# Second feed-forward: h blocks of two chunks by seven products in place of eight

## The chip, the core and the metric

The kernel runs on one core of a Trainium2 chip. The metric is the time of one execution on the device in microseconds (us). Engines: TensorE (PE, with its weight loads as PEld), VectorE (DVE), ScalarE (ACT), GpSimd (POOL) and SyncE (SP), which here issues nearly all DMAs, on one queue.

## The reference, cut to what matters

```python
attn_out = _attn_ref(q, k, v, i_gate, f_gate, o_gate)     # 4 batches, 8 heads, 768 steps, 40 wide
x = attn_out.transpose(0, 2, 1, 3).reshape(3072, 320)
x = (sigmoid(x @ w_gate) * (x @ w_val)) @ w_out           # first feed-forward, 1536 wide
h = x @ w_in                                              # second feed-forward, 2048 wide
g = h * clip(h + 3, 0, 6) / 6
return g @ w_out2                                         # all in float32
```

The change touches `h = x @ w_in` alone, and what has to be at hand for it.

## The kernel before, in words

The 768 steps are cut into 6 chunks of 128; one chunk holds the 512 tokens of four batches. The matmuls take float32 in a form (fp32r) that keeps part of the bits, so each operand is split into a high part (a ScalarE cast) and a low part (a VectorE subtraction), and a product is made of high x high, high x low and low x high.

The first part of the program runs 82 steps, chunk by chunk. Each step computes an h block of the first feed-forward (`m1_h`, 512 columns, L553 to L560), then the output product of the step before (`outputs_but`, `m1_out`), and one piece of the attention of the next chunk (`att0`, `att1`, `att2`). The first two chunks are cut into half blocks; chunks 3 to 6 have 12 steps each, and the sixth has no attention beside it. What VectorE does in a step: the product of gate and value (L580), the low split (L567), and of the attention the decay scans (L387), the weighing (L402) and the outputs' scaling. `work` adds jobs to the steps: it fetches weights as 64-bit words, turns them into float32 (`to_f32`: ScalarE, then VectorE L117 and L120) and, for the second feed-forward, stores them in DRAM (`store_w2`, w2_dram). In the sixth chunk and the first part of the second feed-forward `work` loads them again and splits them into SBUF slots: `split_in` for the h product, `split_out2` for the output product.

The second feed-forward (L844 to L858) runs over 6 chunks and, in each, 8 blocks of two times 128 features. `m2_h(c, n)` makes 2 x 8 matmuls of 512 columns (two blocks of 128 rows with three terms each, the tail of 64 rows in two matmuls) into two PSUM banks of the pool mm_ps; the gate is a ScalarE Relu (L806) and a VectorE product with h (L807), then comes the split (L566, L567). `m2_out(c, n - 1)` follows: 24 matmuls of 320 columns into four banks that sum over all features. `x_split(c + 1)` loads the next chunk's x from x2_dram and splits it.

The eight PSUM banks are three of mm_ps, three of acc_ps and two of att_ps. A planner in the framework orders each engine's instructions when the program is built: by the order in which they are written, and by when their inputs and buffers come free by its own estimates. At run time each engine takes its instructions in that fixed order; so does the DMA queue of SP, where a store that waits for its data holds up the loads behind it. `issue_after(gate)` keeps what is written in it behind that step's gate on the gate's engine.

## Time and profile before

| | |
|---|---|
| runs | 868.65, 869.58 and 872.16 us, median 869.58 |
| profiled execution, first to last instruction | 867.3 us (its span; 2.3 us less than the median) |
| TensorE busy | 842.9 us, 97% |
| VectorE busy | 497.8 us, 57% |
| ScalarE busy | 353.3 us, 41% |
| moved by DMA | 83.4 MB |

The page gives busy shares in 40 slices of the span (about 21.7 us each), the chain of work that ended last, and groups of instructions with their mean duration. Durations of matmuls overlap: the next starts before the last has ended. The windows give each engine's busy time in a stretch; time in which two instructions of one engine overlap counts once there.

### The profile page before, as it was taken

To read this page: it belongs to the slowest core of one execution; us is meant where nothing else is said; L and a number is where in the kernel's file an instruction comes from. 1 tells how busy PE (TensorE), PEld (TensorE's weight loads), DVE (VectorE), ACT (ScalarE), POOL (GpSimd) and SP (SyncE) were. 2 spreads that over 40 slices of the span, in tenths; PEclk is the share of its full clock that TensorE was granted. 3 is DMA by queue.
4 is the path that set the end of the run, shared out by engine and by line. 5 is a ranking of instruction groups with operands and counts; after the bars stand their busy time and mean duration, and the time that the engine had idled before them with its cause. 6 is when DMAs were issued, how large, how long until landed. Compare 5 with 4: busy or idle time off the path is not lost.

```text
span 867.3 us, 16991 instructions
## 1 busy us (share of the span) xinstructions
PE 842.9 (97%) x7205; PEld 727.1 (84%) x7205; DVE 497.8 (57%) x898; ACT 353.3 (41%) x721; POOL 2.5 (0%) x8
## 2 busy tenths in 40 slices
PE   6599899999999999999999999999999999999998
PEld 6488689888878887878888888999999999999997
DVE  8899975765666666667535544344343343443432
ACT  3687743232333343342225445343343343433332
POOL 1000000000000000000000000000000000000000
PEclk9599999999999999999999999999999999999999
DMA  9636723422544555344104221001020020000000
GB/s 350 236 123 212 255 73 109 145 73 73 199 133 157 170 184 186 122 163 169 32 1 149 90 68 73 1 31 37 1 68 1 1 67 1 31 1 1 31 1 30
DMA packets 24923, 83.43 MB, mean 96 GB/s; under 512 B 2576, under 2 KB 5840, under 8 KB 24848
## 3 DMA queue, kind: packets, MB, share of 16 engines
q1 hardware_dynamic: 24800, 82.26, 27.7%
q8 instruction: 56, 0.92, 0.4%
q14 instruction: 19, 0.16, 0.0%
q10 hardware_dynamic: 48, 0.10, 0.0%
HBM read 68.35 MB, written 13.99 MB: 95 GB/s over the span
## 4 chain that ended last, share of the span: by engine, by line
PE 92%; DVE 5%; DMA 1%; issue 1%; ACT 0%; DVEq 0%
PE mm L557 12%; PE mm L559 12%; PE mm L558 12%; PE acc L595 11%; PE mm L553 7%; PE mm L560 6%; PE acc L827 5%; PE acc L826 5%; PE acc L825 5%; PE acc L605 4%; PE att L361 3%; PE att L454 2%; PE att L443 2%; PE att L827 2%; PE att L825 2%; PE att L826 2%
## 5 line engine op out<-in xcount | busy, mean ns | idle before, releaser
L557 PE MATMUL mm<-xh,w 128*128 128x512 f32 (+1 forms) x520 | 195.5, 376 | 0.0
L559 PE MATMUL mm<-xh,w 128*128 128x512 f32 (+1 forms) x520 | 194.8, 375 | 0.0
L558 PE MATMUL mm<-xl,w 128*128 128x512 f32 (+1 forms) x520 | 194.7, 374 | 0.0
L566 ACT CAST gh<-g 128x512 fp32r<-128x512 f32 (+1 forms) x178 | 106.0, 596 | 193.5 <-DVE g L580 98.5
L567 DVE TENSOR_TENSOR gl<-g,gh 128x512 fp32r<-128x512 f32 (+1 forms) x178 | 117.5, 660 | 94.5 <-ACT gh L566 93.5
L807 DVE SCALAR_TENSOR_TENSOR g<-g,mm 128x512 f32<-128x512 f32 x96 | 65.8, 685 | 133.8 <-ACT g L806 133.8
L806 ACT ACTIVATE g<-mm,half 128x512 f32<-128x512 f32 x96 | 65.8, 685 | 133.0 <-PE mm L560 132.9
L559 PEld LDWEIGHTS mm<-xh,w 128*128 128x128 f32 x520 | 98.1, 189 | 18.7
L558 PEld LDWEIGHTS mm<-xl,w 128*128 128x128 f32 x520 | 98.1, 189 | 18.5
L557 PEld LDWEIGHTS mm<-xh,w 128*128 128x128 f32 x520 | 98.3, 189 | 14.2
L553 PE MATMUL mm<-xl,w 128*128 128x512 f32 (+1 forms) x260 | 104.0, 400 | 2.5 <-DVE cst L524 1.6
L595 PE MATMUL acc<-gh,w 128*128 128x512 f32 (+1 forms) x328 | 104.0, 363 | 0.0
L560 PE MATMUL mm<-xh,w 128*128 128x512 f32 (+1 forms) x260 | 97.2, 374 | 0.0
L827 PE MATMUL acc<-w,gl 128*128 128x320 f32 x288 | 89.0, 309 | 0.0
L826 PE MATMUL acc<-w,gh 128*128 128x320 f32 x288 | 88.9, 309 | 0.0
L825 PE MATMUL acc<-w,gh 128*128 128x320 f32 x288 | 88.8, 308 | 0.0
L580 DVE TENSOR_TENSOR g<-g,mm 128x512 f32<-128x512 f32 (+1 forms) x82 | 50.5, 616 | 61.9 <-PE mm L560 61.9
L579 ACT ACTIVATE g<-mm 128x512 f32<-128x512 f32 (+1 forms) x82 | 44.6, 544 | 69.1 <-PE mm L560 67.6
L595 PEld LDWEIGHTS acc<-gh,w 128*128 128x128 f32 x328 | 60.4, 189 | 9.9
L387 DVE TENSOR_TENSOR_SCAN dec<-dec,ident 128x512 f32<-128x512 f32 x40 | 48.2, 1217 | 26.7 <-DMA dec<-fz_dram 26.7
L595 PE MATMUL acc<-gl,w 128*128 128x512 f32 (+1 forms) x164 | 59.7, 364 | 0.0
L553 PEld LDWEIGHTS mm<-xl,w 128*128 128x128 f32 x260 | 49.1, 189 | 12.2 <-DVE cst L524 2.0
(155 smaller groups left out, 1077.8 us busy)
## 6 DMA issues: line engine op xcount, KB each, us to landing
raw<-in_w SPq DMA_DIRECT2D x20, 640.0 KB, 4.1
qk<-in_qkT SPq DMA_DIRECT2D x22, 512.0 KB, 4.4
vko<-in_vko SPq DMA_DIRECT2D x22, 480.0 KB, 4.6
dec<-fz_dram SPq DMA_DIRECT2D x20, 512.0 KB, 5.8
raw<-in_wo SPq DMA_DIRECT2D x14, 640.0 KB, 4.0
w_dram<-bits SPq DMA_DIRECT2D x16, 320.0 KB, 2.4
raw<-w_dram SPq DMA_DIRECT2D x16, 320.0 KB, 2.9
x_dram<-x SPq DMA_DIRECT2D x6, 768.0 KB, 3.2
```

Source lines behind the costliest of these rows:

```text
L553: nc.tensor.matmul(out=banks[j], lhsT=tail, rhs=xl[:, 2, :], start=True, stop=False)
L557: nc.tensor.matmul(out=banks[j], lhsT=hi, rhs=xh[:, k, :], start=False, stop=False)
L558: nc.tensor.matmul(out=banks[j], lhsT=hi, rhs=xl[:, k, :], start=False, stop=False)
L559: nc.tensor.matmul(out=banks[j], lhsT=lo, rhs=xh[:, k, :], start=False, stop=False)
L560: nc.tensor.matmul(out=banks[j], lhsT=tail, rhs=xh[:, 2, :], start=False, stop=True)
L566: nc.scalar.copy(out=gh, in_=g)
L567: nc.vector.tensor_tensor(out=gl, in0=g, in1=gh.bitcast(F32), op=ALU.subtract)
L595: nc.tensor.matmul(out=a[m], lhsT=lhsT, rhs=rhs, start=st and lhsT is hi and rhs is gh, stop=en and lhsT is lo, skip_group_check=True,)
L806: nc.scalar.activation(out=g[j], in_=banks[j], func=AF.Relu, scale=1.0 / 6.0, bias=half)
L825: nc.tensor.matmul(out=a, lhsT=gh[:, ts], rhs=hi, start=st, stop=False)
L826: nc.tensor.matmul(out=a, lhsT=gh[:, ts], rhs=lo, start=False, stop=False)
L827: nc.tensor.matmul(out=a, lhsT=gl[:, ts], rhs=hi, start=False, stop=en)
```

## The change

For a pair of chunks and two feature blocks, h is a 2 x 2 matrix of blocks: feature block by chunk. The 320 rows of the contraction are cut into two halves of 160 (128 and a tail of 32). Strassen's scheme, in Winograd's form, makes the four blocks from 7 products of sums of blocks in place of 8 products of blocks. A product is 4 matmuls: three for the 128 rows, and one for the tail, whose four terms stand on four groups of 32 rows.

- `combine_w2` makes the sums of the weights and their splits on VectorE and ScalarE, once for each of the 8 blocks, at odd steps of the fourth and fifth chunk, and stores them (1.38 MB a block) in ws_dram. `load_group` loads them for each pair of chunks again: 24 loads.
- `x_load` and `x_combine` load the x of two chunks and make its sums and splits, in a main and a tail part: for the first pair in the sixth chunk of the first feed-forward, for the others in the second half of the pair before. `x_split` is gone, and the splits of w_in (`split_in`) with it.
- The order of the second feed-forward becomes: for each of 3 pairs, 8 blocks with 7 products each and the output product of the pair's first chunk between them; then the second chunk's 16 output blocks, whose gated values have been kept in the slots that w_in held.
- The first and the third product are copied from PSUM by ScalarE, and further products are added to them there by the matmuls (bank px or pw, accumulating) and by VectorE (`add_to`). The banks come from `four`: three of a pool and one of att_ps in turn.
- Pools of the first part are closed before the sixth chunk, and a pool `late` takes their room.

```diff
...
+    ws_dram = dram.tile([F2 // 2, P, 7, 3 * P], F32, name="ws_dram")
...
-    def x_split(c):
-        x2 = xpool.tile([P, 3, T], F32, tag="x2", name="x2")
-        nc.sync.dma_start(out=x2, in_=x2_dram[c])
-        x_tiles((2, c))
-        nc.scalar.copy(out=XH[2, c], in_=x2)
-        nc.vector.tensor_tensor(
-            out=XL[2, c], in0=x2, in1=XH[2, c].bitcast(F32), op=ALU.subtract
-        )
...
-    for n in range(F2):
+    for n in [*range(0, F2, 2), *range(1, F2, 2)]:
         jobs.append(((wo2 if n % 2 else w2)[n // 2], store_w2, n))
-    n_conv = len(jobs)
-    for n in range(F2):
-        key = ("out2" if n % 2 else "in2", n // 2)
-        jobs.append((w2_dram[n], split_out2 if n % 2 else split_in, key))
     jobs.reverse()
     def work(count, limit):
...
+    def load_out2(n):
+        x = xpool.tile([P, 640], F32, tag="x2", name="w2f")
+        nc.sync.dma_start(out=x, in_=w2_dram[2 * n + 1])
+        split_out2(("out2", n), x)
+    A11, A12, A21, A22, S1, S2, S4 = range(7)
+    S3 = A21
+    def combine_w2(n):
+        src = w2_dram[2 * n]
+        a = cpool.tile([P, 7, 2, P], F32, tag="wa", name="wa", bufs=1)
+        nc.sync.dma_start(
+            out=a[:, 0:4, 0, :], in_=src[:, 0:512].rearrange("p (ik c) -> p ik c", c=P)
+        )
+        tail = src[:, 512:640].rearrange("(ik r) c -> r ik c", r=32)
+        for r in range(0, P, 32):
+            nc.sync.dma_start(out=a[r : r + 32, 0:4, 1, :], in_=tail)
+        for to, x, y, op in (
+            (S1, A21, A22, ALU.add),
+            (S2, S1, A11, ALU.subtract),
+            (S3, A11, A21, ALU.subtract),
+            (S4, A12, S2, ALU.subtract),
+        ):
+            nc.vector.tensor_tensor(out=a[:, to], in0=a[:, x], in1=a[:, y], op=op)
+        for k, m in ((0, 4), (4, 3)):
+            st = xpool.tile([P, 4, 3, P], F32R, tag="x2", name="ws")
+            sf = st.bitcast(F32)
+            nc.scalar.copy(out=st[:, :m, 0:3:2, :], in_=a[:, k : k + m])
+            nc.vector.tensor_tensor(
+                out=st[:, :m, 1, :], in0=a[:, k : k + m, 0, :], in1=sf[:, :m, 0, :], op=ALU.subtract
+            )
+            for r in (32, 96):
+                q = slice(r, r + 32)
+                nc.vector.tensor_tensor(
+                    out=st[q, :m, 2, :], in0=a[q, k : k + m, 1, :], in1=sf[q, :m, 2, :],
+                    op=ALU.subtract,
+                )
+            nc.sync.dma_start(
+                out=ws_dram[n, :, k : k + m, :],
+                in_=sf[:, :m].rearrange("p s t c -> p s (t c)"),
+            )
+    w_groups = []
+    def load_group(n):
+        t = xpool.tile([P, 7, 3, P], F32R, tag="x", name="wg")
+        nc.sync.dma_start(
+            out=t.bitcast(F32).rearrange("p s t c -> p s (t c)"), in_=ws_dram[n]
+        )
+        w_groups.append(t)
...
+    xsets = []
+    combined = 0
+    def x_load(pair):
+        def rows():
+            return late.tile([P, T], F32, tag="c", name="xr", bufs=11)
+        main, tail = {}, {}
+        for k in range(2):
+            for j in range(2):
+                src = x2_dram[2 * pair + j]
+                main[k, j], tail[k, j] = rows(), None
+                nc.sync.dma_start(out=main[k, j], in_=src[:, k, :])
+        return pair, main
+    def x_combine(loads, tail):
+        pair, b = loads
+        if tail:
+            b = {}
+            for k in range(2):
+                for j in range(2):
+                    b[k, j] = late.tile([P, T], F32, tag="c", name="xr", bufs=11)
+                    for r in range(0, P, 32):
+                        nc.sync.dma_start(
+                            out=b[k, j][r : r + 32],
+                            in_=x2_dram[2 * pair + j, 32 * k : 32 * k + 32, 2, :],
+                        )
+        else:
+            xsets.append(
+                {
+                    key: late.tile([P, 3, T], F32R, tag="X", name="X", bufs=7)
+                    for key in ("B11", "B21", "T1", "T2", "B22", "T3", "T4")
+                }
+            )
+        xs = xsets[-1]
+        b11, b12, b21, b22 = b[0, 0], b[0, 1], b[1, 0], b[1, 1]
+        def put(key, v):
+            x = xs[key]
+            xf = x.bitcast(F32)
+            if tail:
+                nc.scalar.copy(out=x[:, 2, :], in_=v)
+                nc.vector.tensor_tensor(
+                    out=x[64:, 2, :], in0=v[64:], in1=xf[64:, 2, :], op=ALU.subtract
+                )
+            else:
+                nc.scalar.copy(out=x[:, 0, :], in_=v)
+                nc.vector.tensor_tensor(out=x[:, 1, :], in0=v, in1=xf[:, 0, :], op=ALU.subtract)
+        def minus(x, y, out=None):
+            out = late.tile([P, T], F32, tag="c", name="xr", bufs=11) if out is None else out
+            nc.vector.tensor_tensor(out=out, in0=x, in1=y, op=ALU.subtract)
+            return out
+        put("B11", b11)
+        put("B21", b21)
+        t1 = minus(b12, b11)
+        put("T1", t1)
+        t2 = minus(b22, t1)
+        put("T2", t2)
+        put("B22", b22)
+        put("T3", minus(b22, b12, b12))
+        put("T4", minus(b21, t2))
...
             with tc.issue_after(gate):
-                work(c > 1 and f % 2 == 0, n_conv)
+                work(c > 1 and f % 2 == 0, n_jobs)
+                if c > 2 and f % 2 and combined < F2 // 2:
+                    combine_w2(combined)
+                    combined += 1
         elif f == 0:
-            work(F2, n_conv)
+            assert not jobs and not pieces and combined == F2 // 2
+            early_sb.close()
+            late = ctx.enter_context(tc.tile_pool(name="late", bufs=1, reuse_waits="tile"))
+            x_loads = x_load(0)
+            load_group(0)
         else:
-            work(f > 1, n_jobs)
-        if c == NC - 1 and f == 6:
-            x_split(0)
+            if f > 1 and f - 2 < F2 // 2:
+                load_out2(f - 2)
+            if f in (2, 5):
+                x_combine(x_loads, f > 2)
+    taken = [0]
+    def four(odd):
+        taken[0] += 1
+        return ps_att() if taken[0] % 4 == 0 else (ps_acc if odd else ps_mm)()
+    def product(ps, w, s, x, first):
+        for i, (a, b) in enumerate(((2, 2), (0, 1), (1, 0), (0, 0))):
+            nc.tensor.matmul(
+                out=ps, lhsT=w[:, s, a, :], rhs=x[:, b, :], start=first and i == 0, stop=i == 3,
+                skip_group_check=True,
+            )
+    def sbuf_copy(ps):
+        t = late.tile([P, T], F32, tag="c", name="c", bufs=11)
+        nc.scalar.copy(out=t, in_=ps)
+        return t
+    def add_to(t, ps):
+        nc.vector.tensor_tensor(out=t, in0=ps, in1=t, op=ALU.add)
+        return t
+    def gate2(g, h):
+        nc.scalar.activation(out=g, in_=h, func=AF.Relu, scale=1.0 / 6.0, bias=half)
+        nc.vector.scalar_tensor_tensor(
+            out=g, in0=g, scalar=1.0, in1=h, op0=ALU.min, op1=ALU.mult
+        )
+    def gated_split(h):
+        g = gpool.tile([P, T], F32, tag="g", name="g")
+        gate2(g, h)
+        return split_g(g)
     acc2 = {}
-    def m2_h(c, n):
-        banks = [ps_mm(), ps_mm()]
-        h_pair(slots["in2", n], (2, c), banks)
-        gs[c, n] = []
-        g = [gpool.tile([P, T], F32, tag="g", name="g") for _ in range(2)]
-        for j in range(2):
-            nc.scalar.activation(out=g[j], in_=banks[j], func=AF.Relu, scale=1.0 / 6.0, bias=half)
-            nc.vector.scalar_tensor_tensor(
-                out=g[j], in0=g[j], scalar=1.0, in1=banks[j], op0=ALU.min, op1=ALU.mult
-            )
-        for j in range(2):
-            gs[c, n].append(split_g(g[j]))
-    def m2_out(c, n):
-        if n == 0:
-            acc2[c] = [ps_acc(), ps_acc(), ps_acc(), ps_att()]
+    def m2_out(c, n, j, gg):
+        if n == 0 and j == 0:
+            acc2[c] = [(ps_mm, ps_acc)[(c // 2 + c) % 2 ^ 1]() for _ in range(3)] + [ps_att()]
         w = slots["out2", n]
-        gg = gs.pop((c, n))
-        for j in range(2):
-            gh, gl = gg[j]
-            hi, lo = w[:, j, 0:320], w[:, j, 320:640]
-            st, en = n == 0 and j == 0, n == F2 // 2 - 1 and j == 1
-            for t in range(B):
-                ts = slice(t * L, (t + 1) * L)
-                a = acc2[c][t][:, :DM]
-                nc.tensor.matmul(out=a, lhsT=gh[:, ts], rhs=hi, start=st, stop=False)
-                nc.tensor.matmul(out=a, lhsT=gh[:, ts], rhs=lo, start=False, stop=False)
-                nc.tensor.matmul(out=a, lhsT=gl[:, ts], rhs=hi, start=False, stop=en)
+        gh, gl = gg
+        hi, lo = w[:, j, 0:320], w[:, j, 320:640]
+        st, en = n == 0 and j == 0, n == F2 // 2 - 1 and j == 1
+        for t in range(B):
+            ts = slice(t * L, (t + 1) * L)
+            a = acc2[c][t][:, :DM]
+            nc.tensor.matmul(out=a, lhsT=gh[:, ts], rhs=hi, start=st, stop=False)
+            nc.tensor.matmul(out=a, lhsT=gh[:, ts], rhs=lo, start=False, stop=False)
+            nc.tensor.matmul(out=a, lhsT=gl[:, ts], rhs=hi, start=False, stop=en)
...
-    for c in range(NC):
-        for n in range(F2 // 2):
-            m2_h(c, n)
-            if n > 0:
-                m2_out(c, n - 1)
-            elif c > 0:
-                m2_out(c - 1, F2 // 2 - 1)
-                m2_end(c - 1)
-            else:
+    NG = F2 // 2
+    for pair in range(NC // 2):
+        ca, cb = 2 * pair, 2 * pair + 1
+        xs = xsets.pop(0)
+        kept = []
+        prev = None
+        for n in range(NG):
+            if n + 1 < NG:
+                load_group(n + 1)
+            w = w_groups.pop(0)
+            px = four(pair % 2)
+            product(px, w, A11, xs["B11"], True)
+            c11 = sbuf_copy(px)
+            pz = four(pair % 2)
+            product(pz, w, A12, xs["B21"], True)
+            g0 = gated_split(add_to(c11, pz))
+            pw = four(pair % 2)
+            product(pw, w, S1, xs["T1"], True)
+            c22 = sbuf_copy(pw)
+            product(px, w, S2, xs["T2"], False)
+            c12 = sbuf_copy(px)
+            if prev is not None:
+                m2_out(ca, n - 1, 0, prev[0])
+            elif pair == 0:
                 outputs_but(0)
-            if c == 0:
-                work(2, n_jobs)
-            if n == 4 and c + 1 < NC:
-                x_split(c + 1)
-    m2_out(NC - 1, F2 // 2 - 1)
-    m2_end(NC - 1)
+            product(pw, w, S4, xs["B22"], False)
+            add_to(c12, pw)
+            gb = wpool.tile([P, 2, T], F32, tag="w", name="gb", bufs=18)
+            gate2(gb[:, 0], c12)
+            product(px, w, S3, xs["T3"], False)
+            add_to(c22, px)
+            gate2(gb[:, 1], c22)
+            if prev is not None:
+                m2_out(ca, n - 1, 1, prev[1])
+            product(px, w, A22, xs["T4"], False)
+            prev = [g0, gated_split(px)]
+            kept.append(gb)
+            if n == NG - 2 and pair + 1 < NC // 2:
+                x_loads = x_load(pair + 1)
+        more = pair + 1 < NC // 2
+        for j in range(2):
+            m2_out(ca, NG - 1, j, prev[j])
+        m2_end(ca)
+        if more:
+            load_group(0)
+        for n in range(NG):
+            for j in range(2):
+                m2_out(cb, n, j, split_g(kept[n][:, j]))
+            if more and n in (0, 2):
+                x_combine(x_loads, n > 0)
+        m2_end(cb)
```

## Rows read from the trace of the kernel before

**Rows 1.** The page: busy us, share, instructions; then busy tenths of 40 slices.

```profile
PE 842.9 (97%) x7205; PEld 727.1 (84%) x7205; DVE 497.8 (57%) x898; ACT 353.3 (41%) x721; POOL 2.5 (0%) x8
...
PE   6599899999999999999999999999999999999998
...
DVE  8899975765666666667535544344343343443432
...
PEclk9599999999999999999999999999999999999999
DMA  9636723422544555344104221001020020000000
```

**Rows 2.** The page: the chain that ended last, shares of the span by engine.

```profile
PE 92%; DVE 5%; DMA 1%; issue 1%; ACT 0%; DVEq 0%
```

**Rows 3.** Groups by form: out<-in, shapes, count | busy us, mean ns | idle before.

```profile
L557 PE MATMUL mm<-xh,w 128*128 128x512 f32 x440 | 172.6, 392 | 0.0
...
L567 DVE TENSOR_TENSOR gl<-g,gh 128x512 fp32r<-128x512 f32 x158 | 109.2, 691 | 87.1 <-ACT gh L566 86.2
...
L566 ACT CAST gh<-g 128x512 fp32r<-128x512 f32 x158 | 98.0, 620 | 173.4 <-DVE g L580 83.0 <-DVE g L807 44.4 <-PE att L827 29.6
...
L825 PE MATMUL acc<-w,gh 128*128 128x320 f32 x288 | 88.8, 308 | 0.0
...
L807 DVE SCALAR_TENSOR_TENSOR g<-g,mm 128x512 f32<-128x512 f32 x96 | 65.8, 685 | 133.8 <-ACT g L806 133.8
```

**Rows 4.** The chain in order of time from 523 us: start us, us, what.

```profile
523.59 0.23 PE mm L553
...
527.00 0.23 PE mm L560
...
534.54 0.15 PE acc L826
...
537.76 0.15 PE att L827
```

**Rows 5.** Groups by form again: other operations of VectorE and ScalarE.

```profile
L541 DVE TENSOR_TENSOR xl<-att,xh 128x384 fp32r<-128x384 f32 x23 | 12.7, 551 | 2.3 <-ACT xh L540 2.3
...
L624 DVE TENSOR_TENSOR xl<-x,xh 128x1536 fp32r<-128x1536 f32 x6 | 10.5, 1758 | 3.4 <-ACT xh L623 3.4
L623 ACT CAST xh<-x 128x1536 fp32r<-128x1536 f32 x6 | 8.8, 1474 | 0.0
...
L567 DVE TENSOR_TENSOR gl<-g,gh 128x256 fp32r<-128x256 f32 x20 | 8.4, 418 | 7.4 <-ACT gh L566 7.3
...
L611 ACT COPY x<-acc 128x512 f32<-128x512 f32 x12 | 7.0, 586 | 6.3 <-PE acc L595 6.0
```

**Rows 6.** Timeline of a second feed-forward block: start us, us, engine, line, operation.

```profile
603.86 0.39 PE L560 MATMUL mm<-xh,w 128*128 128x512 f32 x1
...
604.35 0.69 ACT L806 ACTIVATE g<-mm,half 128x512 f32<-128x512 f32 x1 [3.07 <-PE mm L560]
...
605.07 0.69 DVE L807 SCALAR_TENSOR_TENSOR g<-g,mm 128x512 f32<-128x512 f32 x1 [3.07 <-ACT g L806]
```

**Rows 7.** DMA, 298 to 378 us, then from 523 us: queue's share; KB each, us to landing.

```profile
q1 hardware_dynamic: 3600, 12.85, 48.1%
...
dec<-fz_dram SPq DMA_DIRECT2D x4, 512.0 KB, 6.1
...
x<-x_dram SPq DMA_DIRECT2D x4, 768.0 KB, 4.2
```

**Rows 8.** Windows: stretch, length, busy us (instructions) by engine, clock, DMA share, GB/s.

```profile
40.00:105.00 65.00, 62.40 (x759) 54.28 (x750) 63.27 (x139) 51.52 (x145) 0.00 (x0) 0.98 0.58 203
298.00:377.60 79.60, 79.60 (x877) 63.97 (x876) 52.61 (x96) 28.24 (x58) 0.00 (x0) 1.00 0.49 163
377.60:404.00 26.40, 26.40 (x308) 21.18 (x307) 17.38 (x34) 9.89 (x20) 0.00 (x0) 1.00 0.57 196
404.00:457.00 53.00, 53.00 (x438) 42.59 (x437) 27.07 (x49) 14.34 (x27) 0.00 (x0) 1.00 0.10 33
457.00:522.40 65.40, 65.40 (x289) 53.35 (x288) 33.99 (x57) 32.92 (x60) 0.00 (x0) 1.00 0.31 102
```

More of the change, by code (lines that the diff above doesn't have):

```diff
@@ L50, in mlstm_then_two_gated_ffn @@
     gpool = ctx.enter_context(tc.tile_pool(name="gpool", bufs=2))
+    dram = ctx.enter_context(tc.tile_pool(name="dram", bufs=1, space=DRAM))
+    early_sb = ExitStack()
+    cpool = early_sb.enter_context(tc.tile_pool(name="cpool", bufs=2))
     mm_ps = ctx.enter_context(tc.tile_pool(name="mm_ps", bufs=3, space=PSUM))
@@ L83, in mlstm_then_two_gated_ffn @@
     w2_dram = dram.tile([F2, P, 640], F32, name="w2_dram")
+    ws_dram = dram.tile([F2 // 2, P, 7, 3 * P], F32, name="ws_dram")
     slots = {}
     def fetch(src):
-        r = gpool.tile([P, 640], I64, tag="raw", name="raw", bufs=3)
-        if src.shape == r.shape and src.dtype == I64:
-            nc.sync.dma_start(out=r, in_=src)
-            return r
-        x = r.bitcast(F32)[:, 0:640]
-        nc.sync.dma_start(out=x, in_=src)
-        return x
+        r = cpool.tile([P, 640], I64, tag="raw", name="raw", bufs=3)
+        nc.sync.dma_start(out=r, in_=src)
+        return r
     def scaled(r):
         upper = r.bitcast(I32).rearrange("p (n two) -> p two n", two=2)[:, 1, :]
-        u = gpool.tile([P, 640], F32, tag="u", name="u", bufs=1)
+        u = cpool.tile([P, 640], F32, tag="u", name="u", bufs=1)
         nc.scalar.activation(
@@ L182, in split_out2 @@
         )
[L184 removed]
+    ap = early_sb.enter_context(tc.tile_pool(name="attn", bufs=2))
     XH, XL = {}, {}
@@ L190, in x_tiles @@
     def x_tiles(key):
-        XH[key] = xpool.tile([P, 3, T], F32R, tag="xh", name="xh")
-        XL[key] = xpool.tile([P, 3, T], F32R, tag="xl", name="xl")
+        x = xpool.tile([P, 2, 3, T], F32R, tag="x", name="x")
+        XH[key], XL[key] = x[:, 0], x[:, 1]
     def slot_f32(n, p=P):
```

7 lines of the change are left out of this document (2 added, 5 removed).

## The prediction

> **What bounds the kernel now.** I read the page's busy rows first. TensorE is busy 842.9 of 867.3 us, and in the 40 slices its digit is 9 from the sixth slice to the last but one, with a granted clock of 9 tenths or more from the third; VectorE's digit falls from 6 and 5 to 3 and 4 in the second feed-forward [rows 1]. The chain of work that ended last is TensorE for 92% [rows 2]. So until the last copy out, work taken from TensorE is time gained, as long as no other engine holds it up. The 40 slices also show where another engine nearly does: in the first slices VectorE is the fuller one, and in the attention stages it stands at 6 and 7.
>
> How much a matmul is worth is not its duration. The groups of instructions give 392 ns for a 512-column matmul and 308 ns for a 320-column one [rows 3], but matmuls overlap. The chain in order of time gives the distance from start to start: 15 steps between 523.59 and 527.00, so 0.227 us for 512 columns, and 22 steps between 534.54 and 537.76, so 0.146 us for 320 [rows 4]. A block of the second feed-forward (one chunk, two feature blocks) is 16 x 0.227 + 24 x 0.146 = 7.15 us, and 48 of them are 343 us, which is what the trace shows from 523.4 to the end.
>
> **What TensorE is spared.** Before, two chunks and two feature blocks take 4 x 8 = 32 matmuls of 512 columns. After, 7 products of 4 matmuls each, 28. The output product is unchanged. There are 3 pairs of chunks and 8 blocks, so 24 x 4 = 96 matmuls less, 96 x 0.227 = **21.8 us**. By the durations it would be 96 x 0.392 = 37.6 us, which would be wrong: 0.165 us of each lies under its neighbour. The trace has the same shape and type of matmul before, so nothing of this term is guessed. (The Trainium skill, page TensorE: Matmul & The Clock Gate, section Back-to-back issue gap, gives some 131 ns per matmul for a sustained stream of 512 columns. The rows at full clock say 227 ns. By the page's figure the gain would be 12.6 us, and it speaks against the change; see the rivals.)
>
> **What the product blocks add, and whether it is hidden.** A block of the first chunk of a pair now takes 28 x 0.227 + 24 x 0.146 = 9.9 us of TensorE. VectorE has in it three sums out of PSUM, four gate products, two splits: 9 operations of 0.685 to 0.691 us [rows 3], 6.2 us, 63%. ScalarE has three copies (0.586 us, [rows 5]), four gates (0.69, [rows 6]) and two casts (0.62, [rows 3]), 5.7 us. Both fit, so the question is only latency. From row to row [rows 6]: the last matmul of a bank starts at 603.86, so its slot ends at 604.09; ScalarE starts at 604.35 (0.26 later) and VectorE follows at 605.07.
>
> Three banks are used again inside a block, and TensorE, which runs in order, waits if the reader is late. Counted from the block's start, with one output block of 1.76 us after the fourth and one after the sixth product: the fourth product (2.73) needs the copy of the first (0.91 + 0.26 + 0.59 = 1.76); the fifth (5.4) that of the third (3.6); the sixth (6.3) that of the fourth (4.5); the seventh (8.97) the sum from the sixth (7.22 + 0.26 + 0.69 = 8.2). All have 0.8 us or more to spare, and the output blocks are the cover. Where that cover is gone, in the first block of each pair, which has no earlier output between its sixth and seventh product, the seventh starts at 5.46 and its bank is ready at 6.4 (or 7.7, if VectorE takes the gate product first): 1 to 2.2 us, three times. I take **3 us** (2 to 7).
>
> A bank is also passed from block to block. The last product's bank is free only after its gate and its product with h, 0.26 + 0.69 + 0.03 + 0.69 = 1.67 us after its end; the next block's second product starts 0.91 us after it. If it gets that bank, 0.8 us are lost. The four-bank rotation does that where the bank from the att pool (one of two, the other holding an output sum) comes round to the second product, twice a pair: 6 x 0.8 = 4.8, part of it filled by output matmuls that the planner can put first. I take **2.5 us**; the bounds are 0 and 0.8 x 21 = 17 us, if it happens in every block.
>
> The weights come as 24 loads of 1.38 MB in place of slots kept in SBUF. 768 KB landed in 4.2 us [rows 7], so in proportion 7.5 us, started at a block's beginning and needed 9.9 us later: hidden, with 2.4 us to spare (0.7 us in the very first block, where the buffer comes free only with the first feed-forward's last h). DMA engines are idle there (digits 0 to 2, [rows 1]).
>
> Between a pair's halves 16 output blocks of 1.76 us follow, 28 us. VectorE has 16 splits (11 us) and, twice, x_combine with 11 operations of 0.69 us for the main part and as many for the tail (15 us): 26 of 28 us. Part moves forward into the last product block, since the seven tiles come free one after another there. The three gate chains at the ends of product runs (0.26 + 4 x 0.69, 3.0 us against a cover of 1.76) can be filled by the next chunk's first output. I take **2 us** (0 to 6). x_split (1.76 us of VectorE and 1.47 us of ScalarE six times, [rows 5]) and the split of the eight input blocks vanish; both were off the path, so nothing is gained.
>
> **What the weights' sums cost in the first feed-forward.** This is the term that decides. combine_w2 runs 8 times, at the odd steps of the fourth chunk (six) and at the first two odd steps of the fifth. On VectorE each has four sums of 256 columns (0.418), one subtraction of 512 (0.691) and one of 384 (0.551), and two 32-row tails of each (the same length: the time goes with the columns: [rows 3, 5]): 1.67 + 1.24 + 2.48 = 5.4 us. In the fourth chunk, 298 to 377.6, VectorE is busy 52.6 of 79.6 us; with six times 5.4 that is 85. In the next four steps 17.4 + 10.8 = 28.2 of 26.4 [rows 8]. Together 113.2 us of work for 106.0 us of TensorE: 7.2 us too much. The nearest row for such a load is 40 to 105, where VectorE worked 63.3 of 65 us, 97%, and TensorE still 62.4 [rows 8]. At 97% the excess is 10.3 us. Against that, back-to-back VectorE operations overlap a little, and the busy sum of the windows counts such time once; and from 404 to 457 VectorE has 27.1 of 53 us, so that what the combines leave over there costs nothing. What is queued behind them on VectorE is the gate's product and the low split of the next step, which the output matmuls wait for, and the decays of the attention.
>
> The DMA queue fills up too. In 298 to 378 the SP queue took 48.1% with 12.85 MB [rows 7]. A combine reads 0.5 MB and writes 1.38 MB, six of them 11.3 MB: 90% in proportion. Its stores wait for VectorE on SP, and behind them stand the loads of q, k, v and decays, which have about two steps to spare against 6.1 us to land. The two x2 buffers that the stores hold are also those of m1_end at the next chunk. For VectorE and DMA together I take **6 us** (0 to 16). In the sixth chunk VectorE has 34 of 65.4 us [rows 8] and gets about 10 more, hidden.
>
> **The sum.** On the profiled span: 867.3 - 21.8 + 3 + 2.5 + 2 + 6 = 859.0. The median of the runs is 2.3 us above the span, so **861.3 us**, I say 861, 1% less.
>
> **Rivals.** (1) VectorE bounds the fourth chunk and takes the gain: each of the eight pairs of steps (13.25 us) holds 8.75 + 5.4 = 14.15 us of VectorE work. If it can work only 85% of the time there, being held by waits for ScalarE and for late transfers, a pair lasts 16.6 us, 27 us lost in all, and the time is 869.6 - 21.8 + 27 + 7.5 = 882, slower. The point from which it decides is a pair of 15.1 us, VectorE at 94%. For it: the sum above and 90% of DMA. Against it: 97% in [rows 8] with TensorE nearly full.
> (2) PSUM turnaround in every block: 17 us in place of 2.5, giving 876, or 870 if half. For it: the 1.67 us of reading against 0.91 us of a product, where two products stood before (1.82). Against: the 0.8 us spare counted above and a planner that can put output matmuls between.
> (3) All hidden: only the first blocks' 3 us remain, 851. For it: VectorE's 97% stretch.
> (4) A 512-column matmul that is taken out frees less than its distance, because the stream could have gone closer: at the smallest distance that the rows show, 0.146 us, the 96 are worth 14.0 us and the time is 869. Against it stand 15 equal steps at full clock; I give it 2%. (The page of the Trainium skill named above would put this case at 870, with its 131 ns.)
> The change can't fail to do what it says on TensorE: the count of matmuls is written out in the code.
>
> **How the numbers follow.** Forecast (853 to 865): 0.48. All hidden (below 853): 0.13. Half or more of the gain spent, by (2) or a mild (1) (865 to 874): 0.18, with (4) 0.20. Slower, (1) or (2) in full: 0.19. A measurement of this kernel tells about 0.5% (4.3 us) from no change: faster means below 865.2, slower above 873.9. That gives 0.61, 0.20, 0.19. The range that leaves out 2 in 10 is 850 to 879: below it only a case without any stall, above it (1) at its full price.
>
> **What would show it.** Right: 672 product matmuls 0.227 us apart where there were 768; from the first product to the end some 329 us in place of 341 to 343; VectorE at 95% or more from 298 to 404 and that stretch 3 to 10 us longer; gaps of 1 to 2 us before the seventh product of each pair's first block. Wrong: gaps in every block before the second or the seventh product (2); TensorE idle 15 us or more in the fourth chunk, or waits there for decays that come late (1); no gaps at all (3); or a first product of a block that waits for its weights, which I cost at nothing.

## The result, and the profile after

The changed kernel takes 862.64 us (median of 4 runs, 860.47 to 863.78), the kernel before 869.42 (868.65 to 872.16) on the same chip. The ratio is 0.9916, with a 95% interval from 0.9896 to 0.9937. The forecast was 861, range 850 to 879.

The profiled execution took 860.47 us, the shortest of the four; its span is 858.6, 8.7 us less than the span before. The first thing to read is the page's slices (busy tenths of 40 slices, 21.5 us each), against [rows 1]:

```profile
span 858.6 us, 17204 instructions
PE 829.1 (97%) x7109; PEld 710.1 (83%) x7109; DVE 603.7 (70%) x1086; ACT 413.2 (48%) x821; POOL 2.5 (0%) x8
...
PE   6599899999999999998999999999999999999998
...
DVE  7899975775576678988956734656766668665653
```

TensorE runs 96 matmuls less (7205 before). VectorE does 106 us more: its digits 8, 9, 8, 8, 9 in the slices from about 320 to 430 us are the weights' sums; behind 515 us the digits 4 to 8 are the second feed-forward. One slice of TensorE, the nineteenth, has fallen from 9 to 8.

Where the 8.7 us come from shows when the span is cut where the first feed-forward ends. Its steps are counted from 0 to 81 here; steps 46 to 57 are the fourth chunk, 58 to 69 the fifth. The timeline gives the start of each step's first matmul; for step 81, the kernel before and the changed one:

```profile
510.68 0.40 PE L553 MATMUL mm<-xl,w 128*128 128x512 f32 x1
```

```profile
518.05 0.40 PE L552 MATMUL mm<-x,w 128*128 128x512 f32 x1
```

So 7.37 us are lost by then, and 16.1 are gained behind it. Of the 7.37, 1.1 us are there by step 2, long before anything that the change touches runs; the start of the program differs by up to 1.3 us between the profiled executions here and explains nothing. Nearly all of the rest comes at four places: 1.19 us at step 52, 0.58 at 54, 0.63 at 61 and 3.96 at 62. Between these the two kernels run in step to 0.05 us.

The windows (stretch, length, busy us by engine, clock, DMA share, GB/s) answer to [rows 8]:

```profile
298.00:377.60 79.60, 78.53 (x869) 62.71 (x869) 69.40 (x133) 34.65 (x65) 0.00 (x0) 1.00 0.76 257
377.60:404.00 26.40, 24.02 (x198) 18.19 (x197) 24.35 (x43) 11.26 (x20) 0.00 (x0) 0.94 0.78 266
404.00:457.00 53.00, 53.00 (x526) 42.58 (x526) 37.98 (x74) 18.06 (x32) 0.00 (x0) 1.00 0.39 135
```

VectorE is at 87% and 92%, not at the 97% of the forecast. The sums cost what was worked out (groups of instructions; 41.8 us for 8 blocks, 5.2 each):

```profile
L663 DVE TENSOR_TENSOR wa<-wa 128x256 f32<-128x256 f32 x32 | 12.1, 419 | 2.1 <-DMA wa<-w_dram 1.9
...
L673 DVE TENSOR_TENSOR ws<-wa,ws 32x512 fp32r<-32x512 f32 x16 | 10.9, 684 | 0.2
...
L673 DVE TENSOR_TENSOR ws<-wa,ws 32x384 fp32r<-32x384 f32 x16 | 8.8, 552 | 0.2
...
L668 DVE TENSOR_TENSOR ws<-wa,ws 128x512 fp32r<-128x512 f32 x8 | 5.5, 689 | 1.4 <-ACT ws L667 1.4
...
L668 DVE TENSOR_TENSOR ws<-wa,ws 128x384 fp32r<-128x384 f32 x8 | 4.5, 557 | 0.2
```

But they don't run at the steps where they are written. The four sums of the first block run at 234.9 us, ten steps ahead; all else stands between 312.9 and 428.5 us, mostly one to three steps late, and the last two blocks start only at 407.2 us. So from 298 to 404 us VectorE has 93.8 us of work (69.40 + 24.35), not 113. The largest loss in TensorE's timeline (in brackets the idle time before, and who ended it):

```profile
393.42 0.39 PE L559 MATMUL mm<-x,w 128*128 128x512 f32 x1
396.04 0.55 PE L534 MATMUL att<-ident,yo 128*128 128x128 f32 x3 [2.23 <-DVE dec L401]
...
396.71 0.63 PE L556 MATMUL mm<-x,w 128*128 128x512 f32 x1
397.14 0.63 PE L557 MATMUL mm<-x,w 128*128 128x512 f32 x1
```

The transposes of `att2` (L534) write into a PSUM bank of att_ps whose scores the weighing (L401) has still to read. On VectorE the weighing stands behind one block of sums:

```profile
388.51 1.55 DVE L663 TENSOR_TENSOR wa<-wa 128x256 f32<-128x256 f32 x4
389.98 0.68 DVE L579 TENSOR_TENSOR g<-g,mm 128x512 f32<-128x512 f32 x1
390.84 0.69 DVE L668 TENSOR_TENSOR ws<-wa,ws 128x512 fp32r<-128x512 f32 x1 [0.19 <-ACT ws L667]
391.55 1.38 DVE L673 TENSOR_TENSOR ws<-wa,ws 32x512 fp32r<-32x512 f32 x2
392.96 0.56 DVE L668 TENSOR_TENSOR ws<-wa,ws 128x384 fp32r<-128x384 f32 x1
393.54 1.12 DVE L673 TENSOR_TENSOR ws<-wa,ws 32x384 fp32r<-32x384 f32 x2
394.69 0.69 DVE L566 TENSOR_TENSOR gl<-g,gh 128x512 fp32r<-128x512 f32 x1
395.30 1.28 DVE L401 TENSOR_TENSOR dec<-att,dec 128x512 f32<-128x512 f32 x2
```

Behind the wait the matmuls stand 0.43 us apart where 0.227 is usual, and the windows around it say why (the last three columns are clock, DMA share and GB/s):

```profile
394.00:396.00 2.00, 0.00 (x0) 0.00 (x0) 1.96 (x5) 0.53 (x2) 0.00 (x0) 1.00 1.01 417
396.00:400.00 4.00, 3.83 (x11) 2.62 (x12) 4.00 (x6) 2.36 (x6) 0.00 (x0) 0.57 0.82 284
400.00:404.00 4.00, 3.99 (x17) 2.95 (x17) 2.61 (x5) 1.06 (x2) 0.00 (x0) 1.00 0.53 188
```

After 2.2 us without a matmul the granted clock is at its lower level, 1.2 GHz, for most of 4 us: 4.0 x (1 - 0.57) = 1.7 us. But the clock doesn't set the 3.96 us. A later run, with an eighth product in the second feed-forward, has the same first feed-forward. In its trace the same wait lasts 2.63 us, the clock stays at 1.00, and step 62 is late by the same 3.96 us:

```profile
395.58 0.55 PE L534 MATMUL att<-ident,yo 128*128 128x128 f32 x3 [2.63 <-DVE dec L401]
...
400.74 0.51 PE L604 MATMUL acc<-gh,w 128*128 128x512 f32 x1 [1.56 <-DVE x L615]
```

```profile
396.00:400.00 4.00, 3.18 (x14) 1.96 (x12) 4.00 (x6) 2.35 (x5) 0.00 (x0) 1.00 0.75 237
```

There TensorE waits a second time, for VectorE's L615, which reads the last bank of the chunk before (`m1_end`) and stands behind the same block of sums. In the changed kernel the same two instructions follow each other, with the slow matmuls in the gap:

```profile
400.45 0.69 DVE L615 TENSOR_TENSOR x<-sw,acc 128x512 f32<-128x512 f32 x1
...
401.19 0.50 PE L604 MATMUL acc<-gh,w 128*128 128x512 f32 x1
```

From the transposes to this matmul it is 5.15 us here and 5.16 us there. So the lateness is VectorE's in both, and the lower clock only filled time in which TensorE would have waited.

Behind step 81, all of TensorE's waits that reach 0.2 us are three, at the end of each run of products, as at 605 us:

```profile
605.13 0.31 PE L959 MATMUL att<-w,gl 128*128 128x320 f32 x1
606.24 0.42 PE L957 MATMUL acc<-w,gh 128*128 128x320 f32 x1 [0.80 <-ACT gh L565]
```

The products themselves take as long as before (336 + 168 + 168 = 672 of them in three groups, mean 391 to 395 ns, [rows 3]), and none of these waits is a product's for its weights: the loads of 1344 KB took 5.7 us to land.

### The profile page after: what moved, and what is told of

Same layout as the page of the kernel before. It is cut to its first block, busy times and chain, and to the rows that moved or that the text cites. A ratio compares the mean times of both kernels' runs of the same rounds, so it can differ in the third digit from the quotient of the medians.

```text
span 858.6 us, 17204 instructions
## 1 busy us (share of the span) xinstructions
PE 829.1 (97%) x7109; PEld 710.1 (83%) x7109; DVE 603.7 (70%) x1086; ACT 413.2 (48%) x821; POOL 2.5 (0%) x8
## 4 chain that ended last, share of the span: by engine, by line
PE 79%; DVE 13%; DMA 4%; issue 2%; ACT 1%; SPq 0%; DVEq 0%; ACTq 0%
PE acc L594 9%; PE mm L920 9%; PE mm L558 6%; PE mm L556 6%; PE mm L557 6%; PE att L920 4%; PE acc L920 4%; PE mm L552 4%; PE acc L604 3%; PE mm L559 3%; PE mm L959 2%; PE mm L957 2%; PE acc L957 2%; PE mm L958 2%; PE acc L959 2%
## 5 line engine op out<-in xcount | busy, mean ns | idle before, releaser
L565 ACT CAST gh<-g 128x512 fp32r<-128x512 f32 (+1 forms) x130 | 76.4, 588 | 132.2 <-DVE g L579 110.4
L556 PE MATMUL mm<-x,w 128*128 128x512 f32 (+1 forms) x328 | 121.0, 369 | 0.0
L557 PE MATMUL mm<-x,w 128*128 128x512 f32 (+1 forms) x328 | 120.8, 368 | 0.0
L558 PE MATMUL mm<-x,w 128*128 128x512 f32 (+1 forms) x328 | 120.4, 367 | 0.0
L566 DVE TENSOR_TENSOR gl<-g,gh 128x512 fp32r<-128x512 f32 (+1 forms) x130 | 84.1, 647 | 51.2 <-ACT gh L565 50.8
L920 PE MATMUL mm<-X,wg 128*128 128x512 f32 x336 | 84.3, 391 | 0.0
L579 DVE TENSOR_TENSOR g<-g,mm 128x512 f32<-128x512 f32 (+1 forms) x82 | 50.4, 615 | 34.6 <-PE mm L559 34.2
L920 PEld LDWEIGHTS mm<-X,wg 128*128 128x128 f32 x336 | 61.9, 188 | 12.6 <-DVE g L936 0.3
L557 PEld LDWEIGHTS mm<-x,w 128*128 128x128 f32 x328 | 62.8, 191 | 10.7
L558 PEld LDWEIGHTS mm<-x,w 128*128 128x128 f32 x328 | 62.6, 191 | 10.6
L556 PEld LDWEIGHTS mm<-x,w 128*128 128x128 f32 x328 | 62.8, 191 | 8.4
L552 PE MATMUL mm<-x,w 128*128 128x512 f32 (+1 forms) x164 | 66.8, 408 | 2.5 <-DVE cst L523 1.6
L578 ACT ACTIVATE g<-mm 128x512 f32<-128x512 f32 (+1 forms) x82 | 44.5, 543 | 44.0 <-PE mm L559 41.8
L386 DVE TENSOR_TENSOR_SCAN dec<-dec,ident 128x512 f32<-128x512 f32 x40 | 48.0, 1215 | 21.3 <-DMA dec<-fz_dram 21.3
L559 PE MATMUL mm<-x,w 128*128 128x512 f32 (+1 forms) x164 | 59.9, 365 | 0.0
L935 ACT ACTIVATE gb<-c,half 128x512 f32<-128x512 f32 x48 | 34.6, 724 | 44.0 <-DVE c L931 43.7
L566 DVE TENSOR_TENSOR gl<-gb,gh 128x512 fp32r<-128x512 f32 x48 | 32.4, 690 | 24.2 <-ACT gh L565 24.1
L565 ACT CAST gh<-gb 128x512 fp32r<-128x512 f32 x48 | 29.5, 620 | 36.5 <-PE att L958 35.1
L920 PE MATMUL att<-X,wg 128*128 128x512 f32 x168 | 46.3, 395 | 0.0
```

The lines of the kernel that those rows point to most:

```text
L386: nc.vector.tensor_tensor_scan(out=x, data0=a["factors"][n] if "factors" in a else x, data1=ident4.rearrange("p h l -> p (h l)"), initial= ...
L552: nc.tensor.matmul(out=banks[j], lhsT=tail, rhs=xl[:, 2, :], start=True, stop=False)
L556: nc.tensor.matmul(out=banks[j], lhsT=hi, rhs=xh[:, k, :], start=False, stop=False)
L557: nc.tensor.matmul(out=banks[j], lhsT=hi, rhs=xl[:, k, :], start=False, stop=False)
L558: nc.tensor.matmul(out=banks[j], lhsT=lo, rhs=xh[:, k, :], start=False, stop=False)
L559: nc.tensor.matmul(out=banks[j], lhsT=tail, rhs=xh[:, 2, :], start=False, stop=True)
```

## The experiments

Four theories of the 6.3 us lost at steps 37 to 62. V: VectorE has too much work in that stretch. D: the transfers, 76 to 78% of the DMA engines against 49 and 57%, come late. P: the loss has nothing to do with the sums, but with buffers and pools. L, formed after the first four runs: VectorE's order decides, that is, at which attention piece a block of sums stands. Four more runs test the terms of the second feed-forward. All times are medians of 4 to 7 runs, with the kernel before measured beside them at 869.7 to 870.2 us.

### The sums alone in the kernel before

```diff
+                if c > 2 and f % 2 and combined < F2 // 2:
+                    combine_w2(combined)
+                    combined += 1
```

> The kernel before, with the weights' sums made and stored at the same steps as in the changed kernel, and nothing that uses them; the second feed-forward is the old one. The order in which w_in and w_out are converted is that of the changed kernel. Theories V and D: the first part's loss of 6 to 7.5 us comes with the sums alone, 875 to 877. Theory P: 869 to 871.

Measured: 877.83 us, ratio 1.0096 (1.0080 to 1.0113), 8.1 us more than before, just above the 875 to 877 of V and D. The losses stand at the same steps as in the changed kernel: 1.88 us at 52, 0.60 at 54, 0.67 at 61, 3.97 at 62, and 0.96 at 37 besides. P falls. Taken from here, the rest of the change is worth 877.83 - 862.64 = 15.2 us.

### More VectorE work, and more transfers

```diff
-            nc.vector.tensor_tensor(out=st[:, :m, 1, :], ...)
+            for _ in range(3):
+                nc.vector.tensor_tensor(out=st[:, :m, 1, :], ...)
```

> The low parts of the 128 rows of each block of sums are computed three times in place of once: 2 x (0.689 + 0.557) = 2.5 us more of VectorE for each of 8 blocks, 20 us in all, no DMA more. Theory V: VectorE, at 87 to 92% in the stretch, is asked for 7.7 us per pair of steps beyond the 8.75, 16.5 of 13.3; 8 to 20 us more than the changed kernel, 871 to 883. Theory D: VectorE has room, at most 2 us more, 865.

Measured: 872.93 us, 10.3 more than the changed kernel, inside what V expected and beyond D's 865. Step 81 is 20.6 us late in this execution. VectorE's work is thus what the loss grows with; by itself that doesn't tell fullness from place.

```diff
             nc.sync.dma_start(out=ws_dram[n, :, k : k + m, :], in_=...)
+            nc.sync.dma_start(out=ws_copy[n, :, k : k + m, :], in_=...)
```

> Each block of summed weights is stored twice, the second time to another place in DRAM that nothing reads: 11 MB more to write between 298 and 430 us, no VectorE work more. Theory V: VectorE's order is what counts, so at most 1 or 2 us more than the changed kernel's 862.6 (864 at most). Theory D: the DMA queue, at 76% in this stretch, would be asked for 100% or more, and loads for the attention land later: 867 or more.

Measured: 865.39 us (861.29 to 868.13), 2.8 more, between the two. The trace is of the shortest execution, 861.29 us, so what makes the others longer isn't in it. In this trace the DMA engines are 94% busy from 377.6 to 404 us, and TensorE doesn't wait there at all (26.40 busy of 26.40). One wait of 4.88 us follows at 404, for the same weighing, and VectorE's timeline has the sums before it again:

```profile
405.01 1.11 DVE L674 TENSOR_TENSOR ws<-wa,ws 32x384 fp32r<-32x384 f32 x2
...
408.61 1.29 DVE L402 TENSOR_TENSOR dec<-att,dec 128x512 f32<-128x512 f32 x2
```

So a DMA queue at 94% doesn't by itself stop TensorE. How much of the 2.8 us is late transfers, and how much the other order that the planner gave this kernel, can't be told.

### The sums at other steps

```diff
-                if c > 2 and f % 2 and combined < F2 // 2:
+                if c > 1 and f % 4 == 3 and combined < F2 // 2:
```

> The weights' sums are made at every fourth step from the third chunk on, not at every second step from the fourth. The changed kernel lost 7.4 us in its first 82 steps against the kernel before, most of it where output matmuls of the attention waited for VectorE, which had the sums' operations queued ahead. Theory V (VectorE too full): in four steps VectorE then has 2 x 8.75 + 5.2 = 22.7 us of 26.5, 86%; the 6.3 us lost behind step 51 go down to 2 or less, and the time is 857 to 859. Theory D (transfers late by a full DMA queue): the DMA load is thinned in the same way, so the same 857 to 859; this run alone doesn't tell V from D. Theory P (the loss is not from the sums but from the other buffers and pools): 862 to 863, no change against the changed kernel.

Measured: 862.55 us, nothing gained: a miss for V and for D as they were put. (It is what P expected, which falls with the run of the sums alone.) The windows of this kernel show that VectorE did get emptier, 77% and 80%, and TensorE waits all the same:

```profile
218.00:298.00 80.00, 77.19 (x855) 61.00 (x855) 61.76 (x120) 30.35 (x60) 0.00 (x0) 0.98 0.66 212
298.00:377.60 79.60, 76.97 (x858) 61.54 (x855) 63.88 (x120) 29.88 (x60) 0.00 (x0) 1.00 0.69 223
```

The losses: 1.28 us at step 37 (before the first sums run), then 3.9 at 40 to 42, 3.0 at 53 and 55, 1.9 at 65 and 67. What TensorE waits for has changed, though. Its two longest waits, 1.82 us at step 41 and 2.14 at step 53, are for a low split of the attention's (L540). Only 0.4 us of sums stand before that on VectorE; the scan ahead of it has itself waited, 2.32 and 2.82 us, for its load of decays. For step 41:

```profile
243.39 2.64 SPq L677 DMA_DIRECT2D ws_dram<-ws  x2
...
250.52 0.94 SPq L220 DMA_DIRECT2D dec<-fz_dram  x1
...
257.38 2.34 DVE L386 TENSOR_TENSOR_SCAN dec<-dec,ident 128x512 f32<-128x512 f32 x2 [2.32 <-DMA dec<-fz_dram]
...
263.08 0.82 PE L453 MATMUL att<-vi,dec 128*32 128x41 f32 x64 [1.82 <-DVE x L540]
```

SP issues this load, the twelfth of 20, at 250.52 us, behind two stores of sums and three other transfers in its order; in the changed kernel it goes out at 241.82. So late transfers do count here, by their place in SP's order and not by a full queue, and they may have taken back what the emptier VectorE gave; no run separates the two. By written steps, the losses follow the block at the eighth step of each chunk; those at the fourth and the last step cost little or nothing. That suggested L, and with it a wrong guess: that it is the attention's transposes at the fourth step behind which sums are harmless.

```diff
+                if c > 1 and f in (3, 6, 9) and combined < F2 // 2:
```

> In the runs so far the losses stand at single steps: VectorE has a block's sums and splits in its order ahead of the weighing or the low split that TensorE waits for, at steps whose attention piece makes new scores; where the sums were written behind a piece that transposes outputs (the fourth and the last step of a chunk in the run with every fourth step), five of six cost nothing. Here the sums stand only at such steps: the fourth, seventh and tenth of the third, fourth and fifth chunk, until 8 are made. In three steps VectorE has 13.1 + 5.2 = 18.3 of 19.9 us, 92%, so on the whole it is no emptier than in the changed kernel. Theory L (local order): the 6.3 us that the changed kernel loses from step 37 to 62 go down to 2 or less, 856 to 859. Theory V (fullness of VectorE): 862 or more.

Measured: 877.61 us, 15 more than the changed kernel. The guess fell, and with it what L expected; V's bound (862 or more) holds. But V's reason doesn't show over a chunk: VectorE is no fuller than in the run before (76% in both windows), and the loss is far larger.

```profile
218.00:298.00 80.00, 74.21 (x828) 59.02 (x827) 61.02 (x120) 30.16 (x59) 0.00 (x0) 0.96 0.66 213
298.00:377.60 79.60, 76.53 (x855) 60.69 (x854) 60.70 (x111) 29.87 (x58) 0.00 (x0) 0.99 0.65 206
```

TensorE's waits over the whole execution (engine, line, waited for: us in all, times, longest) have changed their releasers; now it is the outputs' scaling (L485, L502) and the low split (L540) that come late:

```profile
...
PE att L534 <- DVE yo L502: 5.6, 3, 2.7
...
PE att L360 <- DVE y L485: 3.8, 3, 1.8
PE att L453 <- DVE x L540: 3.5, 3, 1.9
PE att L534 <- DVE dec L401: 2.3, 3, 1.3
```

Three blocks in each of two chunks in both runs, nearly equal VectorE shares, and 15 us between them: the sum over a chunk doesn't decide. The trace shows two ways in which a block's place does. In the third chunk, the waits of 1.01 us at 270.45 and 2.67 at 295.37 are for outputs' operations that stand right behind a block of sums on VectorE; the wait of 1.87 us at 262.63 begins with a scan that waits 2.84 us for its decays, as in the run before. Which steps are harmful isn't explained: behind all three the next piece is `att1`, and the fourth cost little in the run before. Nor is a fullness over three steps (92% by the expectation, against 86% over four in the run before) excluded.

```diff
+                if (c, f) in ((2, 11), (3, 3), (3, 11), (4, 3), (4, 5), (4, 7), (4, 9), (4, 11)):
```

> The sums stay on VectorE, but stand at the last step of the third chunk, the fourth and last of the fourth chunk, and at five odd steps of the fifth chunk from its fourth step on, where VectorE had 27 of 53 us before. In the three runs with other steps, the fourth cost 0, 0, 1.2 and 1.3 us, the last 0 and the seventh to tenth 1.9 to 5. Theory L (the place against the attention pieces decides): the loss is 3 us or less, 857 to 860. Theory V (the sum of VectorE's work decides): also less, since the fifth chunk has room, 857 to 860. If instead any place costs about 0.8 us a block, as in the changed kernel, no change: 862.

Measured: **856.84 us** (855.52 to 857.92), ratio 0.9850 (0.9835 to 0.9865): the fastest of all, 5.8 us below the changed kernel. Step 81 is 3.3 us late in place of 7.4. In the fifth chunk VectorE is then at 84%, with little harm (its windows, the last column but two is the clock, 1.00 throughout):

```profile
298.00:377.60 79.60, 78.89 (x873) 63.24 (x872) 61.79 (x115) 30.11 (x62) 0.00 (x0) 1.00 0.62 207
...
404.00:457.00 53.00, 51.86 (x432) 41.45 (x431) 44.69 (x88) 19.23 (x33) 0.00 (x0) 1.00 0.62 209
```

V and L had both expected this, so the run confirms the remedy more than a theory. Beside the run with every fourth step it shows that a VectorE share of 84% over a chunk can cost less than one of 77 to 80%. The fifth chunk has less of the attention in it: in the kernel before, 2 scans and 4 weighings fall in the 53 us from 404 to 457, 6 and 6 in those from 325 to 378. That this, and not something else in the order, makes the place a good one isn't shown.

### The sums on GpSimd

```diff
-            nc.vector.tensor_tensor(out=a[:, to], in0=a[:, x], in1=a[:, y], op=op)
+            nc.gpsimd.tensor_tensor(out=a[:, to], in0=a[:, x], in1=a[:, y], op=op)
```

(and so for the three subtractions)

> The ten sums and splits of each block of weights are made by GpSimd, which does next to nothing else; ScalarE's copies, the transfers and the steps are those of the changed kernel. VectorE then has none of the added work. Theory V or L (VectorE's added operations, in whatever order): the 6.3 us lost from step 37 to 62 go to 1 or less and the time is 856 to 858. Theory D (transfers): no change, 861 to 864. If GpSimd's traffic slows VectorE's operations down, VectorE's means of 0.69 us per 512 columns rise and part of the loss stays, 858 to 862.

> As the run with GpSimd, and the sums stand at every fourth step from the third chunk on. If GpSimd takes over 13 us for a block, the steps of the changed kernel are too close for it and this one is the better by up to 2 us; if not, both give the same, 856 to 858. Theory D: transfers are thinned too, so below the other by what they cost.

Measured: 895.28 and 876.91 us. Both expectations missed by far, and on the bad side. The first kernel's groups show the durations: GpSimd takes 1406 ns in the mean for 128 rows of 512 columns and 778 for 256, 11.5 us for a block, and VectorE's scans rise from 1215 to 1416 ns.

```profile
L386 DVE TENSOR_TENSOR_SCAN dec<-dec,ident 128x512 f32<-128x512 f32 x40 | 56.0, 1416 | 24.5 <-DMA dec<-fz_dram 24.5
...
L663 POOL TENSOR_TENSOR wa<-wa 128x256 f32<-128x256 f32 x32 | 24.2, 778 | 278.7 <-DMA wa<-w_dram 278.0
```

Beside that, the orders of other engines wait for GpSimd (the stretch 298 to 457 us; us in all, times, longest). ScalarE's copies of the sums (L667) wait 38.5 us for it, 5.3 for VectorE in the changed kernel; VectorE's low splits wait 19.5 us for ScalarE's casts, 6.1 in the changed kernel. On SP the stores of the sums wait 58.9 us for GpSimd (45.4 for VectorE in the changed kernel), and VectorE waits 12.4 us for loads of the attention that go out on the same queue:

```profile
ACT ws L667 <- POOL wa L663: 38.5, 7, 7.8
...
DVE gl L566 <- ACT gh L565: 19.5, 15, 7.8
DVE vi L351 <- DMA vko<-in_vko: 12.4, 3, 6.2
```

```profile
SPq L677 <- POOL ws L673: 58.9, 14, 5.6
```

How the 33 us divide among these isn't shown.

So these runs don't measure VectorE freed of the sums; they replace one order by a worse one.

### The terms of the second feed-forward

```diff
             product(pz, w, A12, xs["B21"], True)
+            product(pz, w, A12, xs["B21"], True)
```

> The second product of each block is made twice into the same bank (the second time it starts anew): 4 matmuls more in each of 24 blocks, so 32 as before the change, with everything else as in the changed kernel. Price by the distance from start to start: 96 x 0.227 = 21.8 us more, 884. By the duration of 392 ns: 37.6 more, 900. By the smallest distance (0.146): 14 more, 877; by the 131 ns of the page TensorE: Matmul & The Clock Gate: 12.6 more, 875.

Measured: 883.43 us, 20.8 more than the changed kernel: 0.217 us for each of the 96 matmuls. Behind step 81 alone the two profiled executions differ by 22.0 us (362.6 and 340.5), 0.230 each. The distance from start to start is the price (0.227); the duration (37.6) and the smaller figures (12.6, 14) are out.

```diff
-        return ps_att() if taken[0] % 4 == 0 else (ps_acc if odd else ps_mm)()
+        return (ps_acc if odd else ps_mm)()
```

> The products rotate over three PSUM banks, without the one of att_ps. A block's first or second product then always takes a bank that the block before has just used; the last product's bank is free only 1.67 us after its end, against 0.91 us of one product. If TensorE keeps the written order: 0.8 us or more in each of 21 blocks, 17 us more, 880. If the planner fills the wait with output matmuls and later products: at most 3 us more, 863 to 866.

Measured: 861.98 us, no more than with four banks. TensorE waits for no bank there either: other matmuls fill the gap, as expected of the planner.

```diff
-        for j in range(2):
-            m2_out(ca, NG - 1, j, prev[j])
+        m2_out(ca, NG - 1, 0, prev[0])
+        first = split_g(kept[0][:, 0])
+        m2_out(cb, 0, 0, first)
+        m2_out(ca, NG - 1, 1, prev[1])
```

> At the end of each run of products the first output block of the pair's second chunk is written ahead of the last output block of its first chunk. In the changed kernel's trace TensorE stands idle there for 0.96, 0.96 and 0.61 us, since the last gated product's chain of 3 us has 1.76 us of cover. With 3.5 us of cover the three waits go: 2.5 us less, 860.1. If the planner already had put all it could there, no change, 862.6.

Measured: 862.08 us, no difference. The three waits are still there, with 0.80, 0.80 and 0.46 us to their names (0.80, 0.80 and 0.45 in the changed kernel): this change of the written order doesn't move them. What would fill them stays open.

## Why the prediction was right

**The saving** of 21.8 us by the distance of [rows 4] holds: 20.8 when the eighth product is put back, 22.0 behind step 81. The rival with a smaller price falls with it, and so does the 131 ns of the Trainium skill's page TensorE: Matmul & The Clock Gate, section Back-to-back issue gap, for these matmuls. One reading beside it was wrong: the second feed-forward of the kernel before doesn't start at 523.4. Its first h block is at 516.1, ahead of the last two output products of the first feed-forward; with their 3.6 us taken off it lasts 344 us, and 327.7 in the changed kernel, 16.3 less.

**The second feed-forward's additions** were put at 7.5 us and came to 5.5 (21.8 - 16.3), but from other places. The 3 us for the first block of each pair: nothing, since the planner sets a product of the next block (the one into a bank of att_ps) ahead of the seventh:

```profile
530.81 1.99 PE L920 MATMUL mm<-X,wg 128*128 128x512 f32 x8
532.63 1.07 PE L920 MATMUL att<-X,wg 128*128 128x512 f32 x4
```

The 2.5 us for banks handed on: nothing, and rival (2) falls with the run of three banks. Both steps failed in the same words, that TensorE takes the written order. The 2 us at the ends of the product runs: 2.5 measured. The remaining 3 us lie in spacings that each exceed the usual one by less than 0.2 us, which no term foresaw. So 5.5 us too much and 3.5 too little were put down; that the sum came within 2 us is in part luck.

**The sums in the first feed-forward** were the term that decides: 6 us forecast, 6.3 measured in the changed kernel's shortest execution and 8.1 in the run of the sums alone. The cost of a block (5.4 forecast, 5.2 measured) was right, and so was the engine: operations behind the sums on VectorE come late. The operations were not those named (the gate's product, the low split, the decays) but the weighing and `m1_end`'s L615, and TensorE waits for them through PSUM banks. The reason for the size was wrong: 113 us of VectorE work in 106 never came about, because two of the eight blocks ran after 404 us and the share from 298 to 404 us was 88%. That 6 us came out all the same is luck: other places for the same blocks cost 0 to 15 us more or 5.8 less (856.84 to 877.61 us). The DMA queue came to 76%, not 90%; that a load can still be late by its place in SP's order was named as a danger, and it shows in the run with every fourth step.

**Rival (1)** at its full price didn't happen in the changed kernel, but a loss like its 27 us is in reach: the worst steps on VectorE cost 15 us more than the changed kernel, and the wrong engine 33. **The weights' loads**, costed at nothing, were: 5.7 us to land where 7.5 was worked out (7.35, with both sizes in KB). **Rival (2)** at half its price is 867, not 870: 8.5 us in place of 2.5. **All hidden (3)**, 851 us, was the better end, and the late steps come to 856.84.

Of the signs of being right, the 672 products 0.227 us apart came. From the first of them to the end it is 335 us, not 329; 3.6 of these are the first feed-forward's last two output products, which stand behind it. VectorE at 95% and the gaps before the seventh products did not come.

## What to carry to other kernels

The gain of a cheaper algorithm on the bounding engine is the number of matmuls saved times their distance from start to start, and that term can be read off before anything is built. What it pays for it isn't told by the helper engine's share over a long stretch (76% in the placing that took 877.61 us, 84% in the fullest stretch of the one that took 856.84): it depends on what stands behind each block of helper work in the fixed orders of the engines and the queue. Look at two of them: the helper engine's, for the operation that the bounding engine waits for next (here the weighing, whose bank the transposes need), and the DMA queue's, for loads behind the block's stores. Then try other places and measure; here the stretch with less of the attention in it was the best.

## What the runs showed of the hardware

The clock: in the changed kernel a wait of 2.23 us was followed by a granted clock of 0.57 in the next 4 us, and in the run with every fourth step one of 1.82 us (mean clock 0.57 from 264 to 268 us, matmuls 0.43 us apart). The same wait, 2.63 us long, in the run with the eighth product was not, nor one of 1.87 us at 262 us in the run with three steps to a chunk, nor one of 0.97 us at 335 us in the changed kernel. So the length of a wait doesn't tell here whether the clock falls. Nor is the lower clock always a loss: at step 62 the lateness was 3.96 us with it and without it.

GpSimd slows VectorE, and some of its own operations take longer beside VectorE's. With GpSimd at work the scans' mean of 1215 ns became 1416 and the low split's 689 became 741. The single operations say more: in the first run with GpSimd, 9 scans that lay wholly beside its operations took 2058 ns in the mean and 28 beside none of them 1217; for the low split it is 1761 ns (3) and 689 (98). GpSimd's sums of 256 columns take 0.72 to 0.75 us where VectorE is idle and up to 1.07 beside its work. The Trainium skill, page SBUF — State Buffer, section Who interferes with whom, says that a VectorE instruction with two inputs in SBUF contends with a GpSimd instruction that reads SBUF. The scans and splits read two SBUF operands and did slow down; the gate's product, which reads one from PSUM (L579), stayed at 680 ns, and at 670 in the 5 that lay beside GpSimd's work. The trace agrees with the rule.
